# Threshold attention with a feed-forward block on one core: four moves in the order of loads, sums and means

## Chip, cores, metric

One core of a Trainium2 chip. The metric is the device time of one launch in microseconds, as the median of repeated runs.

## What is computed

The reference is attention with a threshold, followed by a layer norm and a feed-forward network with a residual. Cut to what matters (B = H = 8, S = 576, D = 64, model width 512, hidden width 2048):

```python
scores = matmul(q, k^T) / sqrt(64)
scores = where(scores >= max(scores) - tau, scores, -1e9)
attn   = softmax(scores)
x      = matmul(attn, v), heads side by side        # (8, 576, 512)
xn     = (x - mean(x)) / sqrt(var(x) + 1e-6) * g_ln
out    = x + relu(xn @ w_ch1) @ w_ch2
```

q, k, v are 32-bit floats. The two weight matrices come as 64-bit floats, and the kernel turns them into 32-bit ones on the chip.

## The kernel before

**Slots.** The work is cut into 72 slots, 9 for each batch, in one main loop over `n` (L1030 on). A slot of attention takes two heads and 256 of their 576 query rows (slots 0 to 3 of a batch the first 256, slots 5 to 8 the second); slot 4 takes what is left of all heads, the "shared heads". In each slot TensorE makes the scores of four blocks of 128 x 576 in PSUM (`scores`, L408), two blocks each in the tiles `sc0` and `sc1`. VectorE takes the maxima of the first two blocks and then of the other two (`exponentials`, L422); GpSimd makes a threshold from each (L426); ScalarE makes the exponentials (L436). `weights` (L443 and on) masks and sums them on VectorE. They are then turned round, in the first 9 slots by TensorE (`turn_weights`, tiles `tp`, `tr`), later by VectorE and a trip through DRAM (`turn_blocks`, L533, and `fetch`). The value products (`values_of`, L591, L601) follow one or two slots later, and ScalarE copies their result from PSUM to a tile `x` (L614, or L609 for the shared heads).

**Groups.** Each batch gives two groups of 288 tokens. GpSimd adds the features of `x` up as they come (`add_feature`, L643, tile `sum`); TensorE makes the mean by a product with a constant matrix (`mean_of`); VectorE subtracts it (`centre`, L666, tile `xc`). Then the group's feed-forward products begin: `first_part` (tile `p`, 16 times four products and a relu by ScalarE, L795), and the second half: for group 0 plainly (`second_plain`), for all others in seven half-size products of sums and differences (`second_quarters`, tile `seg`; VectorE and GpSimd make the sums, L865).

**Order.** The order of instructions on each engine's queue is the order in which the program issues them; it is written by hand. Every slot has points at which postponed calls run: -3, -2, -1 before the maxima, "copy", and the quarters 0 to 3. `at_quarter(n, i, ...)` puts a call at such a point and `run(n, i)` makes it. `second_part(n, i)` gives out feed-forward products, one at a time from a generator, as many as a share of the room (`ROOM`) allows. `group_ready` places a group's mean, centring and start: `ready(0)` is slot 6 quarter 0, `ready(1)` slot 10 quarter 2. The PSUM tiles of turnings, means and feed-forward products share one pool of two buffers.

**Loads.** All loads after the start are issued by SP in program order: `load_qk` (8 transfers of 72 KB, in pieces of 128 bytes; the single input buffer has to be free, so a load waits for the last transpose that reads it, L369), `load_v` (four transfers in batch 0), and the weight chunks. `Weights.fetch(most)` loads up to `most` of the 32 chunks of 512 KB, if room is free for them. Chunks are converted two per slot: VectorE (L271, L275, L298), ScalarE (L279, L283), GpSimd (L289, and L310 for the gain). `turn(u)` makes q and k ready for the scores: GpSimd scales q (L356), VectorE transposes k and q (L359, L363 or L368, L369). It stands behind the maxima of the slot before.

Of the kernel before, what the change touches and what calls it, by code (L numbers as in the profile page):

```python
# [18 lines left out]
def kernel(  # L19
# [36 lines left out]
    HP = H // 2  # L56
# [68 lines left out]
    def load_v(u):  # L125
        b, hp = units[u]
        vt = ins.tile([128, 2, J, D], F32, tag="v", name="v_in")
        vr = v_rest[hp]
        both = v[b, 2 * hp : 2 * hp + 2]
        if b:  # L130
            nc.sync.dma_start(
                out=vt.rearrange("p h c d -> p h (c d)"),
                in_=both[:, : J * 128].rearrange("h (p c) d -> p h (c d)", c=J),
            )
        for h in range(0 if b else 2):
            nc.sync.dma_start(
                out=vt[:, h], in_=both[h, : J * 128].rearrange("(c p) d -> p c d", p=128)
            )
        for j in range(2):
            nc.sync.dma_start(  # L140
                out=vr[64 * j : 64 * j + 64, j], in_=both[:, J * 128 :].rearrange("h p d -> p h d")
            )
        values_in[u] = (vt, vr)
# [270 lines left out]
    def exponentials(n):  # L414


        neg = small.tile([128, 4], F32, tag="neg", name="neg")
        thr = small.tile([128, 4], F32, tag="thr", name="thr")
        es = e_room[(n + 1) % 2 if n < SLOTS else 0]
        for h in range(2):  # L420
            i = slice(2 * h, 2 * h + 2)
            nc.vector.tensor_reduce(  # L422
                out=neg[:, i], in_=pairs[h],
                axis=AXL.X, op=ALU.max, negate=True,
            )
            nc.gpsimd.tensor_scalar(  # L426
                out=thr[:, i], in0=neg[:, i], scalar1=-1.0, scalar2=low_sb,
                op0=ALU.mult, op1=ALU.add,
            )
            if h == 0:  # L430
                conversion.scale_all()
        run(n, "copy")
        for i in range(4):
            if i == 2:
                yield es, thr
            nc.scalar.activation(es[:, i], blocks[i], func=AF.Exp, bias=neg[:, i : i + 1])  # L436
# [128 lines left out]
    def values_of(b, s, turned_weights):  # L565

        em, er = turned_weights
        at_once = b == 0 and s <= HP
        pv = pv_behind
        if at_once:  # L570
            both = ps_ff.tile([128, 2, 128], F32, tag="ff", name="pv")
            pv = [both[:, j] for j in range(2)]
        if s == HP:
            outs = [
                (hp, hp % 2, pv[hp % 2][:, hp // 2 * 64 : hp // 2 * 64 + 64],
                 lambda t, h, hp=hp: t[:, :, (2 * h + hp // 2) * 32 : (2 * h + hp // 2) * 32 + 32])
                for hp in range(HP)
            ]
        else:
            outs = [  # L580
                (s % (HP + 1), j, pv[j], lambda t, h: t[:, :, 64 * h : 64 * h + 64])
                for j in range(2)
            ]
        banks = [0 if at_once else j for _, j, _, _ in outs]
        firsts = [banks.index(bank) == i for i, bank in enumerate(banks)]
        lasts = [bank not in banks[i + 1 :] for i, bank in enumerate(banks)]
        for c in range(J):
            for (hp, j, dst, pick), first in zip(outs, firsts):
                vt, _ = values_in[b * HP + hp]
                for h in range(2):  # L590
                    nc.tensor.matmul(  # L591
                        dst[64 * h : 64 * h + 64], lhsT=vt[:, h, c, :],
                        rhs=pick(em[:, 2 * j : 2 * j + 2, c], h), start=c == 0 and first, stop=False,
                    )

        def rest():
            for (hp, j, dst, pick), last in zip(outs, lasts):
                _, vr = values_in[b * HP + hp]
                rows = slice(0, 128) if at_once else slice(64 * j, 64 * j + 64)
                for h in range(2):  # L600
                    nc.tensor.matmul(  # L601
                        dst[64 * h : 64 * h + 64], lhsT=vr[rows, j, h],
                        rhs=pick(er[rows], h), start=False, stop=last,
                    )

        def copy(j):
            if s == HP:
                for t in range(2):
                    nc.scalar.copy(  # L609
                        x_of(2 * b + t)[:, :, QH:].rearrange("p (a j) x -> p j a x", j=2)[:, j],  # L610
                        pv[j].rearrange("p (a t x) -> p t a x", a=2, t=2)[:, t],
                    )
            else:
                nc.scalar.copy(  # L614
                    x_of(2 * b + (s > HP))[:, s % (HP + 1), 128 * j : 128 * j + 128], pv[j]
                )

        def add():
            if s == HP:
                for t in range(2):  # L620
                    for c in range(1, NK):
                        add_feature(2 * b + t, c, slice(QH, TOK))
            elif s % (HP + 1):
                add_feature(2 * b + (s > HP), s % (HP + 1), slice(0, QH))

        if at_once:
            rest()
            copy(0)
            copy(1)
            add()  # L630
        else:
            n = b * SLOTS + s + 2
            at_quarter(n, -3, rest)
            at_quarter(n, -2, copy, 1)
            at_quarter(n, "copy", copy, 0)
            at_quarter(n, 0, add)

    def add_feature(g, c, cols):

# [7 lines left out]

    means, centred = {}, {}

    waiting_mean, banks_taken = [], [False]  # L650

    def mean_of(g):
        if banks_taken[0]:
# [289 lines left out]
    QUARTERS = 4  # L943
# [10 lines left out]
    def at_quarter(n, i, fn, *args):  # L954
        later_calls.setdefault((n, i), []).append((fn, args))

    def run(n, i):
        for fn, args in later_calls.pop((n, i), ()):
            fn(*args)

    def ready(g):

        if g < 2:
            return (24, 42)[g]
        b, t = divmod(g, 2)
        return QUARTERS * (b * SLOTS + (HP, 2 * HP)[t] + 2) + (2, 4)[t]

    def second_part(n, i):

        nonlocal issued, owed, part, now  # L970
        part, now = i, QUARTERS * n + i
        if not queue:
            return
        at = QUARTERS * n + i
        g = sum(issued >= e for e in ends)
        left = sum(ROOM[t % QUARTERS] for t in range(at, ready(g + 1))) if g + 1 < NG else 0
        owed += (ends[g] - issued) * ROOM[i] / left if left > 0 else 8


        got = 1 if i in (0, QUARTERS - 1) else 2  # L980
        while queue and (owed >= 0.5 or got == 1 and i in (0, QUARTERS - 1)):
            got, cost = next(queue[0], (None, 0))
            if got is None:
                queue.pop(0)
                got = 1
            elif got == 0:
                owed = 0.0
                break
            else:
                issued += cost  # L990
                owed -= cost

    def group_ready(g):
        first = divmod(ready(g), QUARTERS)
        before = divmod(ready(g) - 1, QUARTERS) if g else (first[0], -1)
        at_quarter(*before, mean_of, g)
        at_quarter(*(first if g and first[1] else before), centre, g)
        at_quarter(*first, lambda: queue.append(ffn_steps(g)))

    conversion = Weights()  # L1000
    if w_ch1.dtype == I64:
        conversion.fetch(4)
    else:
        for i in range(NK):
            nc.sync.dma_start(out=w1_sb[i], in_=w_ch1[i * 128 : (i + 1) * 128])
            nc.scalar.mul(w1_sb[i], w1_sb[i], g_sb[:, i : i + 1])
        for i in range(ND):
            nc.sync.dma_start(
                out=w2_sb[:, :, i],
                in_=w_ch2[i * 128 : (i + 1) * 128, :].rearrange("p (m c) -> p m c", m=NK),  # L1010
            )
        conversion.begun = conversion.carried = len(conversion.chunks)
        conversion.masked = conversion.fetched = conversion.begun
        conversion.scaled = conversion.n1
# [11 lines left out]

    constants(22)
    turn(0)
    load_v(1)
    for n in range(NS):  # L1030
        b, s = divmod(n, SLOTS)
        masks_at, behind_at, end_at = BEGUN[min(n, len(BEGUN) - 1)]
# [67 lines left out]
        if n >= HP + 2:  # L1100
            conversion.mask_all()
        run(n, 3)
        if b == 0 and s < HP - 2:
            load_v(s + 2)
        elif n >= SLOTS - 2 and (n + 2) % SLOTS < HP and n < NS - 2:
            load_v((n + 2) // SLOTS * HP + (n + 2) % SLOTS)
        second_part(n, 3)
# [44 lines left out]
```

## Time and profile before

| | |
|---|---|
| median of 3 runs | 1380.49 us (1380.27 to 1380.86) |
| profiled execution, its own time | 1383.39 us |
| its span, first to last instruction | 1381.4 us |
| VectorE busy | 919.6 us (67%) |
| GpSimd busy | 616.2 us (45%) |
| span of slots 0 to 9, from the first scores to those of slot 10 | 10.06 to 180.05 us |
| one batch later on | 159.1 us (450.6 to 609.7) |
| group 0: mean, first feed-forward product | 82.97, 88.79 us |
| group 1: mean, first feed-forward product | 187.53, 195.79 us |

The profile is one execution. A row of its timeline gives the start, the length, the engine, the line, the operation with the tile it writes and those it reads, how many records are merged in it, and in brackets how long the engine stood idle before it and what ended that. PE is TensorE (PEld its weight loads), DVE VectorE, ACT ScalarE, POOL GpSimd, SP the queue of loads and stores. A product here leaves four records (two halves of the output, each in two passes). Waits for several things are put down to the one that came last.

### The profile page before, as it was taken

The page shows a single profiled execution, that of the slowest core. Times are in us where ns is not written, and L with a number is a line of the kernel's source. Part 1 is how long each engine was busy: PE and PEld are TensorE (multiplying, and loading weights), DVE is VectorE, ACT ScalarE, POOL GpSimd, SP SyncE. Part 2 cuts the span into 40 slices and gives each one's busy share as a digit, 9 for nine tenths or more (in the row PEclk, how much of TensorE's full clock was granted, in tenths as well). Part 3 has the DMA queues.
Part 4 walks back from the last instruction along what each step waited for, and adds up shares of the span by engine and source line. Part 5 has one row for each costly group of instructions (what it writes and reads, how often), then busy time and mean ns, then how long its engine had stood idle before and what let it go on. Part 6 is the DMA issues. An engine that isn't in the chain of part 4 may idle for free.

```text
span 1381.4 us, 40994 instructions
## 1 busy us (share of the span) xinstructions
PE 1334.9 (97%) x17648; PEld 1008.5 (73%) x17648; DVE 919.6 (67%) x1638; ACT 455.1 (33%) x991; POOL 616.2 (45%) x823
## 2 busy tenths in 40 slices
PE   8989989999999999999999999999999999999996
PEld 6756655868778696867768687776868677786966
DVE  5888957676766777667766667657776767766211
ACT  3776523232323323232332323323232323323120
POOL 3464544544534454443444354343444445344313
PEclk9999999999999999999999999999999999999998
DMA  9722455447744576437744477445764476444211
GB/s 181 215 82 87 95 164 159 154 144 189 192 146 148 156 183 198 138 124 196 199 153 148 154 197 192 136 154 168 183 189 139 133 191 180 139 156 143 51 17 18
DMA packets 322020, 206.88 MB, mean 150 GB/s; under 512 B 247984, under 2 KB 279472, under 8 KB 313776
## 3 DMA queue, kind: packets, MB, share of 16 engines
q1 hardware_dynamic: 317072, 203.68, 50.5%
q8 instruction: 138, 2.26, 0.7%
q10 hardware_dynamic: 4736, 0.59, 0.4%
q14 instruction: 42, 0.34, 0.1%
q0 software_dynamic: 32, 0.00, 0.0%
HBM read 120.46 MB, written 83.76 MB: 148 GB/s over the span
## 4 chain that ended last, share of the span: by engine, by line
PE 84%; DVE 7%; ACT 2%; POOL 2%; issue 2%; DMA 2%; SPq 1%; POOLq 0%; DVEq 0%; ACTq 0%
PE p L101 35%; PE seg L101 28%; PE sc L408 9%; PE sc L591 8%; PE sc L601 2%; DVE neg L422 1%; DVE e L443 1%; PE tp L101 1%; DVE w L298 1%; ACT e L436 1%; DVE w L275 1%; PE mean L101 1%; POOL sum L643 1%; SPq L116 1%; POOL q_in L356 1%
## 5 line engine op out<-in xcount | busy, mean ns | idle before, releaser
L101 PE MATMUL p<-xc,w 128*64 128x288 f32 x4096 | 519.9, 409 | 14.1 <-ACT hidden L795 5.1
L101 PEld LDWEIGHTS p<-xc,w 128*64 128x64 f32 x4096 | 288.5, 137 | 223.2 <-issue 15.8
L422 DVE TENSOR_REDUCE neg<-sc 128x2 f32<-128x1152 f32 x144 | 188.6, 1351 | 237.5 <-PE sc L408 237.0
L101 PE MATMUL seg<-hidden,w 128*64 128x144 f32 x3840 | 248.3, 287 | 3.8 <-DVE hidden L865 3.8
L101 PEld LDWEIGHTS seg<-hidden,w 128*64 128x64 f32 x3840 | 234.9, 137 | 15.7 <-issue 7.5
L459 POOL TENSOR_SCALAR e<-e,den 128x576 f32<-128x576 f32 x252 | 193.8, 780 | 115.0 <-DVE den L448 114.7
L443 DVE SCALAR_TENSOR_TENSOR e<-sc,thr,e 128x576 f32<-128x576 f32 x288 | 222.0, 809 | 19.8 <-POOL thr L426 14.9
L426 POOL TENSOR_SCALAR thr<-neg,low_sb 128x2 f32<-128x2 f32 x144 | 42.1, 292 | 418.5 <-DVE neg L422 416.2
L795 ACT ACTIVATE hidden<-p 128x288 f32<-128x288 f32 x256 | 106.3, 416 | 325.2 <-PE p L101 323.5
L436 ACT ACTIVATE e<-sc,neg 128x576 f32<-128x576 f32 x288 | 197.6, 754 | 4.1 <-DVE neg L422 4.1
L533 DVE STREAM_TRANSPOSE et<-e 128x1152 f32<-128x1152 f32 x112 | 153.1, 1373 | 18.2 <-POOL e L459 17.7
L408 PE MATMUL sc<-kT,qT 64*64 64x384 f32 (+3 forms) x2048 | 140.8, 406 | 5.3 <-DVE e L443 5.1
L591 PE MATMUL sc<-em,v_in 128*64 128x128 f32 (+1 forms) x2368 | 129.5, 263 | 0.0
L591 PEld LDWEIGHTS sc<-em,v_in 128*64 128x64 f32 x2368 | 122.9, 137 | 7.8
L101 PE MATMUL seg<-hidden,stage 128*64 128x144 f32 x1920 | 123.3, 286 | 0.0
L101 PEld LDWEIGHTS seg<-hidden,stage 128*64 128x64 f32 x1920 | 117.6, 137 | 2.9 <-issue 2.9
L614 ACT COPY x<-sc 128x128 f32<-128x128 f32 x120 | 31.6, 265 | 241.5 <-PE sc L408 174.7
L408 PEld LDWEIGHTS sc<-kT,qT 64*64 64x64 f32 x2048 | 76.9, 134 | 47.0 <-issue 21.5
L865 POOL TENSOR_TENSOR hidden<-hidden 128x576 f32<-128x576 f32 x60 | 84.7, 1426 | 47.8 <-ACT hidden L795 38.2
L880 ACT COPY part<-seg 128x288 f32<-128x288 f32 x75 | 30.2, 403 | 198.4 <-PE seg L101 194.3
L865 DVE TENSOR_TENSOR hidden<-hidden 128x576 f32<-128x576 f32 x60 | 49.2, 854 | 49.1 <-PE seg L101 46.1
L101 PE MATMUL seg<-hidden,e 128*64 128x144 f32 x960 | 65.3, 286 | 0.0
(149 smaller groups left out, 1141.6 us busy)
## 6 DMA issues: line engine op xcount, KB each, us to landing
scr<-et SPq DMA_DIRECT2D x63, 1152.0 KB, 4.9
em<-scr SPq DMA_DIRECT2D x63, 1024.0 KB, 5.7
out_dram<-ot SPq DMA_DIRECT2D x256, 36.0 KB, 3.7
q_in<-in_q_dram SPq DMA_DIRECT2D x124, 72.0 KB, 2.5
k_in<-in_k_dram SPq DMA_DIRECT2D x120, 72.0 KB, 2.8
er<-scr SPq DMA_DIRECT2D x126, 64.0 KB, 5.2
v_in<-in_v_dram SPq DMA_DIRECT2D x28, 256.0 KB, 5.4
w<-in_moe_w_ch_dram SPq DMA_DIRECT2D x12, 512.0 KB, 5.5
```

The lines of the kernel that those rows point to most:

```text
L101: nc.tensor.matmul(out[r], lhsT=lhsT[:, r], rhs=rhs, **flags)
L408: nc.tensor.matmul(sc[h][64 * i : 64 * i + 64, at : at + n], lhsT=ql[r] if s == HP else qT[r, half, j * 128 + 64 * i : j * 128 + 64 * i + 64],
L422: nc.vector.tensor_reduce(out=neg[:, i], in_=pairs[h], axis=AXL.X, op=ALU.max, negate=True,)
L426: nc.gpsimd.tensor_scalar(out=thr[:, i], in0=neg[:, i], scalar1=-1.0, scalar2=low_sb, op0=ALU.mult, op1=ALU.add,)
L436: nc.scalar.activation(es[:, i], blocks[i], func=AF.Exp, bias=neg[:, i : i + 1])
L443: nc.vector.scalar_tensor_tensor(out=es[:, i], in0=blocks[i], scalar=thr[:, i : i + 1], in1=es[:, i], op0=ALU.is_ge, op1=ALU.mult, accum_o ...
L459: nc.gpsimd.tensor_scalar(out=es[:, i], in0=es[:, i], scalar1=den[:, i : i + 1], scalar2=1.0, op0=ALU.mult, op1=ALU.mult,)
L533: nc.vector.transpose(et[:, :, 64 * h : 64 * h + 64].rearrange("p n (j c) -> p j n c", j=2), es[:, 2 * h : 2 * h + 2].rearrange("p j (n c) ...
L591: nc.tensor.matmul(dst[64 * h : 64 * h + 64], lhsT=vt[:, h, c, :], rhs=pick(em[:, 2 * j : 2 * j + 2, c], h), start=c == 0 and first, stop= ...
L614: nc.scalar.copy(x_of(2 * b + (s > HP))[:, s % (HP + 1), 128 * j : 128 * j + 128], pv[j])
L795: nc.scalar.activation(hidden[:, d], p1, func=AF.Relu)
L865: eng.tensor_tensor(out=out[at], in0=in0[at], in1=in1[at], op=op)
```

## The change

It has four parts, and all of them change only where something stands in the order; what is computed stays the same.

- Loads: three weight chunks instead of four are fetched ahead of the loop, so that each later call fetches one chunk earlier in the list. The second v is loaded in slot 0 quarter 3 instead of ahead of the loop; the third and fourth v also come one slot later.
- Group 0's mean and centring move from point -1 of slot 6, ahead of the maxima, to quarter 0, behind them.
- The point "copy" moves from behind both maxima to behind the first maximum and its threshold, and the add of the features moves from quarter 0 to that point, behind the copy. On GpSimd the add so stands between the two thresholds.
- Group 1's mean and centring move to behind the fourth product of slot 10's quarter 1. Before, the mean stood ahead of that quarter's products and the centring behind the weights.

```diff
             if h == 0:
+                run(n, "copy")
                 conversion.scale_all()
-        run(n, "copy")
...
             at_quarter(n, "copy", copy, 0)
-            at_quarter(n, 0, add)
+            at_quarter(n, "copy", add)
...
-    waiting_mean, banks_taken = [], [False]
+    waiting_mean, banks_taken, among = [], [False], []
...
+        steps = 0
         got = 1 if i in (0, QUARTERS - 1) else 2
         while queue and (owed >= 0.5 or got == 1 and i in (0, QUARTERS - 1)):
...
                 issued += cost
                 owed -= cost
+                steps += 1
+                if steps == 4 and among:
+                    mean_of(among[0])
+                    centre(among.pop())
...
-        before = divmod(ready(g) - 1, QUARTERS) if g else (first[0], -1)
-        at_quarter(*before, mean_of, g)
-        at_quarter(*(first if g and first[1] else before), centre, g)
+        before = divmod(ready(g) - 1, QUARTERS) if g else first
+        if g == 1:
+            at_quarter(*before, lambda: among.append(g))
+        else:
+            at_quarter(*before, mean_of, g)
+            at_quarter(*(first if g and first[1] else before), centre, g)
...
-        conversion.fetch(4)
+        conversion.fetch(3)
...
     turn(0)
-    load_v(1)
...
-        if b == 0 and s < HP - 2:
-            load_v(s + 2)
+        if b == 0 and s < HP - 1:
+            load_v(s + 1)
```

## The prediction

> **What bounds the kernel now.** I read the page's busy shares first, then the chain of work that ended last, then the waits of TensorE, then the timelines of the four places where TensorE stands still and the change acts.
>
> ```profile
> PE 1334.9 (97%) x17648; PEld 1008.5 (73%) x17648; DVE 919.6 (67%) x1638; ACT 455.1 (33%) x991; POOL 616.2 (45%) x823
> PE 84%; DVE 7%; ACT 2%; POOL 2%; issue 2%; DMA 2%; SPq 1%; POOLq 0%; DVEq 0%; ACTq 0%
> ```
>
> TensorE is the bound: only 1381.4 - 1334.9 = 46.5 us of the span are without a matmul, and no edit here removes one. What can be won is idle time of TensorE and time at a lowered clock. In the table by stage a whole batch after the start (450.6 to 609.7) has 157.85 us of TensorE in 159.1, so most of it lies before 240 us. I number slots by the pass of the main loop; slots 0, 1, 2, 6, 10 and 19 start their scores at 10.06, 18.41, 33.80, 78.85, 180.05 and 660.42.
>
> The start, from the timeline of 0 to 38 us (start, length, engine, instruction, idle time before it):
>
> ```profile
> 16.71 0.20 DVE L369 STREAM_TRANSPOSE q_last<-q_in 128x64 f32<-128x64 f32 x1
> 17.75 5.64 SPq L116 DMA_DIRECT2D q_in<-in_q_dram  x4
> 23.44 2.12 SPq L116 DMA_DIRECT2D k_in<-in_k_dram  x4
> 28.48 0.78 DVE L359 STREAM_TRANSPOSE kT<-k_in 128x576 f32<-128x576 f32 x1 [3.79 <-DMA k_in<-in_k_dram]
> 33.80 0.86 PE L408 MATMUL sc<-kT,qT 64*64 64x384 f32 x4 [2.71 <-DVE e L443]
> 35.28 3.49 PE L408 MATMUL sc<-kT,qT 64*64 64x384 f32 x28 [0.61 <-DVE e L443]
> ```
>
> The third q, k are late: VectorE stands 3.79 us for k in slot 1, its weights come late, and the scores of slot 2 wait 2.71 + 0.61 us and then take 3.49 us where slot 1 has 2.16.
>
> Slot 10, where group 1's mean and centring stand:
>
> ```profile
> 186.75 0.72 POOL L643 TENSOR_TENSOR sum<-sum,x 128x256 f32<-128x256 f32 x1
> 187.53 0.71 PE L101 MATMUL mean<-sum,avg_sb 128*64 128x288 f32 x4 [2.79 <-POOL sum L643]
> 188.06 6.22 PE L101 MATMUL p<-hidden,w 128*64 128x288 f32 x36
> 195.79 4.59 PE L101 MATMUL p<-xc,w 128*64 128x288 f32 x36 [1.50 <-DVE xc L666]
> ```
>
> Three losses in a row: 2.79 us for the sum, 36 records in 6.22 us where the 36 below take 4.59, and 1.50 us for the centring.
>
> Slot 19, as an example of one stall per batch, and its row among the waits of TensorE (total, times, longest):
>
> ```profile
> 665.53 0.73 POOL L643 TENSOR_TENSOR sum<-sum,x 128x256 f32<-128x256 f32 x1
> 666.25 0.74 POOL L356 TENSOR_SCALAR q_in<-q_in,scl_sb 128x576 f32<-128x576 f32 x1
> 667.02 0.77 DVE L363 STREAM_TRANSPOSE qT<-q_in 128x256 f32<-128x256 f32 x2 [1.14 <-POOL q_in L356]
> 668.71 4.14 PE L101 MATMUL seg<-hidden,w 128*64 128x144 f32 x64 [0.63 <-DVE hidden L865]
> ```
> ```profile
> PE seg L101 <- DVE hidden L865: 3.8, 6, 0.6
> ```
>
> GpSimd does the sum, then the scaling of q; VectorE's transposes wait 1.14 us for it, and the operand of the fifth product (L865) is 0.63 us late. The chain of waits runs through exactly these steps.
>
> **What the Trainium skill says.** "TensorE: Matmul & The Clock Gate", What's actually happening: an idle window of about 3.4 us halves TensorE's clock until it has been busy as long. The trace agrees on the half (granted clock 0.50 in 36 to 38, 0.57 in 188 to 192) but shows it after gaps of only 2.71 + 0.61 and 2.79 us. "DMA: Bandwidth & Descriptors", Queues, rings and completion order: each DMA engine takes a queue's descriptors in ring order; the trace agrees in that the second and third q transfers take 2.57 and 1.81 us to issue while what was issued before drains. "PSUM — Partial Sum Buffer", PSUM bank collisions raise a hardware error: engines must not be in one bank at once. That is why the copy of the first half of x waits for the first maximum: 1.07 us in slot 19, from 663.96 on. Same page, Engine vs sequencer instructions: the queues of GpSimd and VectorE are strictly first in, first out, so each instruction moved delays or frees all behind it.
>
> **1. Loads.** Ahead of the third q, k go the fourth weight chunk (0.52 MB) and four transfers of v (0.32 MB). The q issue then waits only for L369 (ends 16.91) instead of 17.75: 0.75 us by issue alone. The backlog shrinks by 0.84 MB; at the 350 GB/s of 16 to 20 us that is 2.4 us. If the stalls go fully, eight issues of 0.5 us from 17.0 end at 21.1, and with the 2.9 us from the end of k's issue to the transpose k is there at 24.0, before VectorE's maxima end (24.68); then q's scaling (0.74, on GpSimd after the thresholds at 25.12) limits, and the transposes end 3.3 us earlier. I take the middle of 2.4 and 3.3: 2.9. TensorE's gap before slot 2 then nearly goes (its fill products end at 31.1, the scores could start at 30.9), so the clock should not fall, and 3.49 becomes 2.16; of that 1.3, VectorE gains what it waits beyond its own work, about 0.9. **Sum 3.8 us**, bounds 0.75 and 4.4. What is moved comes later: the fourth chunk and the first half of slot 0's fetch stand behind k's issue at about 22, land by the median 5.5 us at 28, and are wanted at 35.95 - 2.9 = 33; the second v is issued by 27 and wanted by slot 2's value products at 43.59 - 3.8. Third and fourth v go one slot later and keep a slot's margin. The next q, k stand behind the same number of bytes as now. SP's queue carries no other work there. Cost: nothing.
>
> **2. Group 0 (slot 6).** Mean and centring go from ahead of the maxima to behind them. Now TensorE waits 0.78 us for the sum, its four turnings are torn by the mean's PSUM bank, VectorE waits 1.32 us, and the first product stands at 88.79. After: turnings straight behind the scores (end 82.19); in slot 7 the last copy ends 4.35 us after the scores, so 86.54; mean 0.5, first subtraction 0.45, 0.14 to start: 87.7. **Gain 1.0 us.** Against it: VectorE idles from the maxima's end (85.1) to the mean and starts its weights 0.9 us later; their second half waits 2.63 us for exponentials today, which covers it. Bounds: a loss of 0.3 to a gain of 1.5.
>
> **3. Group 1 (slot 10).** Four of the 9 products of quarter 1 go ahead of the mean. They cover 4 x 4 x 0.12 = 1.9 us of the 2.79; the sum goes ahead of the second threshold, 0.7 us sooner (part 4), and covers the rest. So products to 186.4, mean 0.48, five more of 0.48: 189.3, with the pipe's end 189.6 instead of 194.28. The lowered clock (6.22 against 4.6 at the pace below) goes too. Centring then stands ahead of the weights on VectorE and starts behind the transposes and the mask of the last chunk, at about 189.8; the bank of the next product is free 0.5 us after 189.6. First product of group 1 at 190.2 instead of 195.79: **5.6 us**, bounds 4.0 (clock falls a little) and 6.3. VectorE's weights come 1.5 us later; the scores of slot 11 that overwrite their input stand at 203.78 - 5.6 = 198.2, weights end near 194.5. Slots 11 and 12 are a chain of VectorE from slot 11's maxima on, which wait for scores and so move along.
>
> **4. Sums (each later slot with features).** GpSimd's add goes between the two thresholds. In slot 19: first threshold 664.04, copy done 664.23, sum 664.35 to 665.08, second threshold at 665.30 as before, q's scaling at 665.53 instead of 666.25. VectorE gains 0.72, which covers the 0.63 that TensorE waits. Six times: **3.8 us**, bounds 0 and 4.4. Where copies are late (slot 8: 139.91) nothing is won. In the slot of the shared heads six small adds of 0.25 to 0.29 don't fit: the second threshold comes 0.77 us later, the weights with it (they wait for it 0.47 already), and the centring starts at 758.1 instead of 757.40; its product stands at 758.74 for a PSUM bank and needs 0.45 + 0.14 after that start, so it just fits. Cost taken 0, up to 0.5 in 7 batches.
>
> **Sum.** 3.8 + 1.0 + 5.6 + 3.8 = 14.2. From the profiled execution's 1383.39 that makes 1369.2; that execution is 2.9 above the median of the runs, so the median 1380.49 goes to **1366.3**.
>
> **Rivals.** (a) Issue of the third q, k keeps its pace (their 128-byte pieces, not the backlog, make the 2.57 and 1.81): part 1 gives 0.75, time 1369.3. For: even later issues take 0.5 us each; against: no other group has such stalls. (b) What slot 10 wins is handed back before slot 12, because VectorE and GpSimd (weight differences, L772) are behind there: TensorE waits 1.97 us at 228.49 and the clock falls again. Without part 3: 1371.9. For: the chain is VectorE's from 205.93 to 226.59; against: it begins at scores. (c) Another wait takes the place of L865 in each batch, since the weight load of the same product names a PSUM copy (0.86 us): without part 4, 1370.1. (d) **Slower:** every fetched chunk stands one place later, and VectorE, in order, stands still for each. Price 6.7 us a time, as at 182.36 where one late chunk holds it; four slots make 26.8, less the 14.2: 1393. It decides from 3.6 us a slot on; the margin is 5 us at median landing, and the longest landing of a chunk is 10.4, so it would need all four near the worst. (e) The chunk order happens to end the wait at 182.36: 1.6 us more, 1364.7.
>
> **Numbers.** Forecast 0.56, (a) 0.16, (b) 0.12, (c) 0.10, (d) 0.03, (e) 0.03. The range 1363 to 1372 holds all but (d) and mixtures. A measurement of this kernel can tell about 0.2% from no change (2.8 us); faster by more 0.94, within 0.03, slower 0.03.
>
> **What would show it.** Step 1: VectorE's wait for k in slot 1 under 1 us, slot 2's scores in 2.2 us. Step 2: first product of group 0 about 1 us nearer to slot 6's scores. Step 3: no wait of a mean for the sum, granted clock 1.00 in slot 10, first product of group 1 about 10 us after slot 10's scores start instead of 15.7. Step 4: the L865 wait of TensorE gone, VectorE's wait for q at 0.4 us. I am wrong if slots 3 to 9 become longer, or if second thresholds come later in ordinary slots.

## The result and the profile after

| | before | after |
|---|---|---|
| median | 1380.67 us (1380.27 to 1383.31, 4 runs) | 1367.22 us (1367.01 to 1368.69, 4 runs) |
| ratio, 95% interval | | 0.9901 [0.9884, 0.9918] |
| profiled execution, its span | 1383.39, 1381.4 us | 1367.01, 1365.0 us |

The kernel is 13.5 us (1.0%) faster; the forecast was 14.2. A second set of four runs of after, on another occasion, gave 1366.95 us and 0.9895 [0.9882, 0.9907].

From the page of after, the busy line and the shares of the chain that ended last:

```profile
PE 1330.1 (97%) x17648; PEld 1007.4 (74%) x17648; DVE 921.5 (68%) x1638; ACT 455.3 (33%) x991; POOL 616.7 (45%) x823
PE 88%; DVE 4%; ACT 3%; POOL 1%; issue 1%; DMA 0%; POOLq 0%; DVEq 0%; ACTq 0%; SPq 0%
```

TensorE now stands 1365.0 - 1330.1 = 34.9 us instead of 46.5; its busy time fell by 4.8 as well, at the same number of matmuls, because less of it ran at half clock. In the chain TensorE holds 88% instead of 84%, VectorE 4% instead of 7%.

The first scores of each slot cut both traces into stages:

| stage | before | after | gain | predicted |
|---|---|---|---|---|
| to slot 3 | 47.67 | 43.19 | 4.48 | 3.8 |
| slots 3 to 8 (group 0 in slot 6) | 108.35 | 107.59 | 0.76 | 1.0 |
| slot 9 | 24.03 | 24.72 | -0.69 | 0 |
| slot 10 (group 1) | 23.73 | 17.79 | 5.94 | 5.6 |
| slot 11 | 16.59 | 16.59 | 0 | 0 |
| slot 12 | 19.73 | 18.04 | 1.69 | 0 |
| slot 13 to the end | 1141.30 | 1137.08 | 4.22 | 3.8 |

They add up to 16.4, the difference of the two spans. The medians differ by only 13.5, and what lies between has to be explained too. Slot 9 alone became longer, by almost what slots 3 to 8 gained; slots 3 to 9 together stayed as long as they were (132.38 and 132.31 us).

The start of after, from the timeline:

```profile
17.09 3.09 SPq L116 DMA_DIRECT2D q_in<-in_q_dram  x4
20.23 2.12 SPq L116 DMA_DIRECT2D k_in<-in_k_dram  x4
24.71 0.77 DVE L359 STREAM_TRANSPOSE kT<-k_in 128x576 f32<-128x576 f32 x1
31.16 3.14 PE L408 MATMUL sc<-kT,qT 64*64 64x384 f32 x32
```

The issue of the third q (four transfers) takes 3.09 us instead of 5.64, k's transpose has no bracket any more (before: 3.79 us idle), and slot 2's scores begin right behind the fill products. They end at 34.30 instead of 38.77.

Slot 10 of after:

```profile
176.09 0.43 DVE L271 TENSOR_SCALAR stage<-x_room 128x512 uint32<-128x512 uint32 x1 [6.65 <-DMA x_room<-in_moe_w_ch_dram]
177.55 4.59 PE L101 MATMUL p<-hidden,w 128*64 128x288 f32 x36
179.75 0.72 POOL L643 TENSOR_TENSOR sum<-sum,x 128x256 f32<-128x256 f32 x1
181.97 0.66 PE L101 MATMUL mean<-sum,avg_sb 128*64 128x288 f32 x4
183.36 2.16 PE L101 MATMUL p<-hidden,w 128*64 128x288 f32 x16 [0.26 <-DVE w L298]
185.35 4.54 PE L101 MATMUL p<-xc,w 128*64 128x288 f32 x36
```

Nine products (36 records) run ahead of the mean where there were five (20 records), at full clock. The sum ends at 180.47, 1.5 us ahead of the mean that needs it. The first product of group 1 stands 9.85 us behind the slot's first scores (175.50), where before it was 15.74. VectorE still waits 6.65 us for the last weight chunk.

Slot 19 of after, and the row of its transposes among VectorE's waits:

```profile
650.42 8.16 PE L101 MATMUL seg<-hidden,w 128*64 128x144 f32 x128
650.81 0.73 POOL L643 TENSOR_TENSOR sum<-sum,x 128x256 f32<-128x256 f32 x1
651.99 0.74 POOL L356 TENSOR_SCALAR q_in<-q_in,scl_sb 128x576 f32<-128x576 f32 x1
652.76 0.77 DVE L363 STREAM_TRANSPOSE qT<-q_in 128x256 f32<-128x256 f32 x2 [0.45 <-POOL q_in L356]
```
```profile
DVE qT L363 <- POOL q_in L356: 14.5, 28, 1.7
```

The sum stands ahead of the second threshold (651.74), the transposes wait 0.45 us instead of 1.14, and 128 product records follow without a gap. Over the kernel that wait fell from 28.3 to 14.5 us; TensorE's wait for L865 (3.8 us) has no row any more.

### The profile page after: what moved, and what is told of

Its sections match the earlier page's. It is cut to its first block, busy times and chain, and to the rows that moved or that the text cites. A ratio compares the mean times of both kernels' runs of the same rounds, so it can differ in the third digit from the quotient of the medians.

```text
span 1365.0 us, 40999 instructions
## 1 busy us (share of the span) xinstructions
PE 1330.1 (97%) x17648; PEld 1007.4 (74%) x17648; DVE 921.5 (68%) x1638; ACT 455.3 (33%) x991; POOL 616.7 (45%) x823
## 4 chain that ended last, share of the span: by engine, by line
PE 88%; DVE 4%; ACT 3%; POOL 1%; issue 1%; DMA 0%; POOLq 0%; DVEq 0%; ACTq 0%; SPq 0%
PE p L101 35%; PE seg L101 31%; PE sc L408 10%; PE sc L591 8%; PE sc L601 2%; PE tp L101 1%; DVE e L443 1%; ACT e L436 1%; DVE w L298 1%; PE var L101 0%; PE mean L101 0%; DMA x_room<-in_moe_w_ch_dram 0%; DVE neg L422 0%; DVE et L533 0%; DVE w L275 0%
## 5 line engine op out<-in xcount | busy, mean ns | idle before, releaser
L436 ACT ACTIVATE e<-sc,neg 128x576 f32<-128x576 f32 x288 | 197.6, 754 | 4.1 <-DVE neg L422 4.1
L865 POOL TENSOR_TENSOR hidden<-hidden 128x576 f32<-128x576 f32 x60 | 84.8, 1427 | 51.9 <-ACT hidden L795 42.3
L865 DVE TENSOR_TENSOR hidden<-hidden 128x576 f32<-128x576 f32 x60 | 51.2, 887 | 49.1 <-PE seg L101 46.1
```

Source lines behind the costliest of these rows:

```text
L865: eng.tensor_tensor(out=out[at], in0=in0[at], in1=in1[at], op=op)
```

## The experiments

Lengths of stages in us, each from one profiled execution. "Ratio" is against the runs of before made beside the kernel (medians 1380.96, 1380.56 and 1381.04 in three sets), with its 95% interval.

| kernel | median | ratio | to slot 3 | slot 9 | slot 10 | slot 12 | 13 to end |
|---|---|---|---|---|---|---|---|
| before | 1380.67 | | 47.67 | 24.03 | 23.73 | 19.73 | 1141.3 |
| before again | 1382.89 (1 run) | | 47.29 | 24.03 | 23.72 | 19.74 | 1141.2 |
| loads only | 1376.13 | 0.9971 [0.9960, 0.9982] | 43.09 | 24.75 | 21.19 | 19.74 | 1141.3 |
| sums only | 1374.63 | 0.9953 [0.9935, 0.9971] | 46.57 | 24.02 | 20.97 | 19.74 | 1137.1 |
| group 1 only | 1377.07 | 0.9974 [0.9967, 0.9982] | 45.31 | 24.02 | 20.01 | 18.04 | 1141.3 |
| group 0 only | 1378.53 | 0.9989 [0.9980, 0.9997] | 47.52 | 24.03 | 22.29 | 19.74 | 1141.3 |
| v only | 1378.08 | 0.9985 [0.9977, 0.9992] | 44.33 | 24.03 | 22.27 | 18.06 | 1141.3 |
| chunk only | 1376.15 | 0.9972 [0.9962, 0.9981] | 44.22 | 24.81 | 21.16 | 19.75 | 1141.3 |
| after without group 1 | 1369.18 | 0.9922 [0.9907, 0.9937] | 43.16 | 24.73 | 20.01 | 18.06 | 1137.2 |
| fill before slot 2 | 1379.40 | 0.9993 [0.9985, 1.0000] | 44.91 | 24.02 | 22.25 | 18.05 | 1141.3 |
| after, four chunks | 1368.45 | 0.9904 [0.9891, 0.9916] | 43.09 | 24.02 | 18.79 | 19.73 | 1137.2 |
| after, shared adds back | 1367.00 | 0.9899 [0.9884, 0.9914] | 43.10 | 24.73 | 17.78 | 18.05 | 1137.2 |
| after again | 1366.95 | 0.9895 [0.9882, 0.9907] | 43.08 | 24.76 | 17.82 | 18.04 | 1137.1 |

My theory was the prediction's sum, each part acting in its own place. The rivals were that parts share the same time, so that some of it is counted twice, and that part of what the profile of before shows belongs to that one execution.

**Before again** (no edit).

> The kernel before, unchanged, profiled a second time. Theory 1 (the two profiles differ by the change alone): the span is 1381.4 us again and the 52 records of slot 12's feed-forward products take 8.2 us at half clock, as in the first profile. Theory 2 (the first profile of before holds clock losses that most executions don't have, about 2.9 us, the distance of its 1383.4 from the median 1380.5): the span is about 1378.5, those 52 records take 6.5 us as after the change, and one of the other places at half clock (slot 2, slot 10) may also differ.

The second execution has the same three stretches of slow products: 3.85 us for slot 2's 28 score records, 6.22 for 36 records in slot 10, 8.21 for 52 in slot 12. So theory 1 held here; one execution more says little on how often.

**Loads only.**

```diff
-        conversion.fetch(4)
+        conversion.fetch(3)
...
-    load_v(1)
...
-        if b == 0 and s < HP - 2:
-            load_v(s + 2)
+        if b == 0 and s < HP - 1:
+            load_v(s + 1)
```

> Only the loads are moved (three chunks ahead of the loop, second v in slot 0). Theory 1 (each part acts at its place): 4.5 us less up to slot 7, where the trace after the change has 4.47, and nothing later: 1376.2. Theory 2 (the shift by one chunk also changes when the last chunks are converted, so that slot 9 loses 0.7 and slot 10's maxima are no longer held up by the last chunk, which brings the sum 1.6 us sooner): 1373.5 to 1375.5, with the mean's wait in slot 10 at about 1.2 us instead of 2.79.

The start gains all of its 4.6 us here already (47.67 to 43.09). The prediction had nothing later. But slot 9 becomes 0.7 us longer and slot 10 2.5 shorter, 1.5 of it the clock, which stays full there (36 records in 4.54 us); the mean's wait for its sum is 1.8 us instead of 2.8. The median, 1376.13, is theory 1's, the stages are nearer to theory 2, but the last chunk still holds up slot 10's maxima (VectorE waits 6.69 us for it), only less far into the slot.

**v only, chunk only** (each half of the edit above by itself).

> Only the loads of v are moved, four chunks stay ahead of the loop. Theory 1 (backlog in bytes: v is 0.32 of the 0.84 MB that go): about 40% of the start's gain, VectorE's wait for k in slot 1 at 2 us instead of 3.79, time 1378.5. Theory 2 (the number of pieces counts, not the bytes: v's 256-byte rows are most of the pieces ahead of q, k): nearly the whole gain, wait under 0.5 us, 1376.2, and no shift of the later chunks, so that slot 9 is as before.

> Only the fourth chunk is moved, v stays ahead of the loop. Theory 1 (bytes): 60% of the start's gain, wait for k at 1.5 us, plus the effect in slots 9 and 10: 1376 to 1378. Theory 2 (pieces): little at the start, wait for k above 3 us; what is left is the effect of the shifted chunks, slot 9 longer by 0.7 and slot 10's maxima right behind the scores: 1378 to 1380.

From the timeline of v only, then of chunk only:

```profile
19.20 5.04 SPq L116 DMA_DIRECT2D k_in<-in_k_dram  x4
26.47 0.78 DVE L359 STREAM_TRANSPOSE kT<-k_in 128x576 f32<-128x576 f32 x1 [1.72 <-DMA k_in<-in_k_dram]
```
```profile
17.20 4.82 SPq L116 DMA_DIRECT2D q_in<-in_q_dram  x4
26.36 0.78 DVE L359 STREAM_TRANSPOSE kT<-k_in 128x576 f32<-128x576 f32 x1 [1.63 <-DMA k_in<-in_k_dram]
```

With either half k's transpose starts at about 26.4, against 27.05 to 28.48 in the executions with all loads in their old place, and an issue stall stays with either: it moves from q to k when v is gone. The waits, 1.72 and 1.63 us, are near what theory 1 (bytes) said for each half. What lies ahead of the transfers matters, then, which speaks against rival (a), their own 128-byte pieces, the same in all three kernels. But 0.32 and 0.52 MB give about the same, and k's arrival varies by more than a microsecond between executions of the same loads: after with four chunks, below, has the loads of v only up to here, and its k is waited for by 0.57 us alone, as little as theory 2 (pieces) said. Whether bytes or pieces count, and how much each, stays open.

The change of slots 9 and 10 belongs to the chunk alone: 24.81 and 21.16, against 24.03 and 22.27 with v only.

**Sums only.**

```diff
             if h == 0:
+                run(n, "copy")
                 conversion.scale_all()
-        run(n, "copy")
...
-            at_quarter(n, 0, add)
+            at_quarter(n, "copy", add)
```

> Only the adds are moved between the thresholds. Theory 1: six stalls of 0.63 to 0.70 us go, 4.0 us, and the mean of group 1 waits 0.7 us less: 1375.8. Theory 2 (the adds matter only together with the other parts, since something else is late next): 1378 to 1380, with a wait of TensorE for L865 still in the slots 19, 28, ...

Theory 1 held in the later slots: they gain 4.2 us, all that after gains there. Slot 19 is 18.08 us long instead of 18.78, and so is the same slot of the five batches behind it. In slot 10 the mean waits 1.3 us instead of 2.8, a gain of twice the 0.7 expected.

**Group 1 only.**

```diff
+                steps += 1
+                if steps == 4 and among:
+                    mean_of(among[0])
+                    centre(among.pop())
...
+        if g == 1:
+            at_quarter(*before, lambda: among.append(g))
...
```

> Only group 1's mean and centring are moved among the products. Theory 1 (this move alone takes out most of slot 10's losses): the mean waits 1.1 us for the sum instead of 2.79, the clock stays up, first product of group 1 near 191.2 instead of 195.8: 4.6 us, 1375.9. Theory 2 (the gain of slot 10 needs the earlier sum): the clock still falls after the mean and the gain is 2.5 us or less, 1378.

From TensorE's timeline of slot 10 in this kernel:

```profile
185.17 0.71 PE L101 MATMUL mean<-sum,avg_sb 128*64 128x288 f32 x4 [0.85 <-POOL sum L643]
187.76 2.16 PE L101 MATMUL p<-hidden,w 128*64 128x288 f32 x16 [1.40 <-DVE w L298]
```

The move by itself takes 3.7 us off slot 10 as the profile of before has it, between what the two theories said. The wait for the centring is gone and that for the sum is short, but a new one stands behind the mean: 1.40 us for the conversion of the last weight chunk (L298), which VectorE ends behind the late maxima and the transposes. The prediction had that step of VectorE ahead of the centring, but no product that waits for it.

**Group 0 only.**

```diff
-        before = divmod(ready(g) - 1, QUARTERS) if g else (first[0], -1)
+        before = divmod(ready(g) - 1, QUARTERS) if g else first
```

> Only group 0's mean and centring are moved behind the maxima. Theory 1: first product of group 0 stands 0.74 us sooner after slot 6's scores, as in the trace after the change, and all of it stays: 1379.8. Theory 2 (the chain from slot 7 to 10 is VectorE's and a late chunk's, so that the gain is lost before slot 10): 1380.5, with slot 10's scores at the same place as before.

Slots 3 to 8 shrink from 108.35 to 107.57 us, as in after. The medians lie 2.0 us apart, but the interval, 0.4 to 2.8 us, also holds the 0.8 that the stages show. In this profile slot 10 is 22.29 although the mean waits 2.86 us, because the products behind it keep their pace.

**After without group 1** (after with the mean and the centring of group 1 where they were before).

```diff
-        if g == 1:
-            at_quarter(*before, lambda: among.append(g))
-        else:
-            at_quarter(*before, mean_of, g)
-            at_quarter(*(first if g and first[1] else before), centre, g)
+        at_quarter(*before, mean_of, g)
+        at_quarter(*(first if g and first[1] else before), centre, g)
```

> The changed kernel with group 1's mean and centring back at their old places. Theory 1 (that move is worth the 5.6 us put down to it): 1372.8. Theory 2 (earlier sums and the earlier last chunk already bring the sum 2.4 us forward, so the mean waits only 0.4 us and the clock stays up; only the late centring is left): 1.5 to 2.5 us, 1368.7 to 1369.7.

Theory 2 held: 1369.18 us, and the mean waits only 0.3. With the other parts in place the move is worth 2.2 us in slot 10 (20.01 to 17.79), not 5.6.

**Fill before slot 2.**

```diff
-            constants(8 if n > 1 else 26)
+            constants(26 if n == 1 else 20 if n == 2 else 8)
```

> The kernel before with 12 more fill products ahead of slot 2's scores (20 instead of 8), on a tile that nobody reads. Theory 1 (slot 2's slow scores are a lowered clock, brought on by TensorE's idle gap ahead of them): the gap shrinks to under 1.4 us, the 28 score records take 2.16 us instead of 3.5 to 3.85, slot 3 starts about 1.5 us sooner (46 instead of 47.3 to 47.7), and the median goes from 1380.6 to about 1379.2. Theory 2 (the scores are slow since k and q arrive piece by piece): the records stay at 3.5 or more, and the time at 1380.6.

All 32 score records of slot 2 now take 2.37 us, from 33.63 on, and slot 3 starts at 44.91. Of the 2.8 us to before, 1.4 is k, which came that much earlier in this execution (27.05 against 28.48); the rest is the clock, which stayed up. The median fell by 1.6 us, with an interval that just touches no change. So theory 1 holds in the profile: without the gap the clock stays up. That a gap brings it down each time doesn't hold, as group 1 only shows (a gap of 1.60 + 0.61 us there, and 2.16 us for the records). The same execution gives the plainest contrast with before. TensorE's rows of slot 10:

```profile
184.99 0.71 PE L101 MATMUL mean<-sum,avg_sb 128*64 128x288 f32 x4 [2.82 <-POOL sum L643]
185.53 4.54 PE L101 MATMUL p<-hidden,w 128*64 128x288 f32 x36
```

and two stretches of 2 us behind the mean in the table by stage, first of before, then of this kernel (TensorE's busy time and records come first; the granted clock stands behind GpSimd's):

```profile
188.00:190.00 2.00, 2.00 (x12) 1.02 (x10) 1.76 (x6) 0.00 (x0) 0.20 (x1) 0.55 0.01 2
```
```profile
185.00:187.00 2.00, 2.00 (x18) 1.21 (x20) 1.30 (x5) 0.46 (x1) 0.67 (x1) 1.00 0.03 8
```

The same wait, the same code, and once 0.55 of the clock and 6.22 us for the 36 records, once 1.00 and 4.54. The last section shows what differs.

**After, four chunks** (after with `conversion.fetch(4)`).

> The kernel after with four weight chunks instead of three fetched ahead of the loop; the moved v stays. Theory 1 (the shifted chunk order costs 0.7 us in slot 9 and wins about 1.6 us in slot 10, since the last chunk then no longer holds the maximum): slot 9 back to 24.0 us from 24.7, slot 10 at 19 to 19.4 us from 17.79, the start as good within 0.7 us; time 1368 to 1369.5. Theory 2 (the order of the chunks matters only at the start): slots 9 and 10 at 24.7 and 17.8, time 1367.4.

Slot 9 goes back to 24.02 and slot 10 to 18.79: the order of the chunks costs 0.7 in one and gives 1.0 in the other. VectorE's rows ahead of slot 9's maxima, of after (slot from 150.78) and then of this kernel (from 150.69):

```profile
153.18 1.70 DVE L275 SCALAR_TENSOR_TENSOR stage<-stage 128x512 uint32<-128x512 uint32 x1
155.19 2.58 DVE L422 TENSOR_REDUCE neg<-sc 128x2 f32<-128x1152 f32 x2
```
```profile
153.03 2.58 DVE L422 TENSOR_REDUCE neg<-sc 128x2 f32<-128x1152 f32 x2
```

In after a second chunk is begun ahead of the maxima, which start 2.1 us later. The last chunk is converted 6.5 us after its issue in both (169.56 to 176.09, and 169.75 to 176.31) and waited for as long; since slot 10 starts later in after (175.50 against 174.71), the wait lies beside more of its scores. So in slots 9 and 10 the chunk order is worth about 0.3 us. At the start this execution is as good as after (43.09 and 43.19), but that of v only, with the same loads, had k 1.25 us later and slot 3 at 44.33, while the five profiles with both parts of the loads moved all lie at 43.08 to 43.19. The median, 1.2 us higher than after's, doesn't divide this: the profiled run, 1368.80, has slot 12's longer form, 19.73, and a later k would add about as much.

**After, shared adds back.**

```diff
-            at_quarter(n, "copy", add)
+            at_quarter(n, 0 if s == HP else "copy", add)
```

> The kernel after with the six small adds of the shared heads' slot back behind both thresholds, the adds of all other slots left where they are. Theory 1 (part 4 costs nothing in the shared heads' slot, as predicted): within 0.5 us of the kernel after, 1366.7 to 1367.7. Theory 2 (the second threshold, 0.77 us later, is paid in each of seven batches): 3 to 5 us faster, 1362 to 1364. Theory 3 (the adds are needed early there too): slower, 1369 or more.

Theory 1 held: 1367.00 us, and the later slots 1137.2 as in after. The rows of the first weights, the second threshold and the centring in after, in one shared slot, then the centring in this kernel, whose slot stands 0.07 us earlier:

```profile
739.78 0.82 DVE L443 SCALAR_TENSOR_TENSOR e<-sc,thr,e 128x576 f32<-128x576 f32 x1 [0.47 <-ACT e L436]
740.16 0.27 POOL L426 TENSOR_SCALAR thr<-neg,low_sb 128x2 f32<-128x2 f32 x1
743.14 1.52 DVE L666 TENSOR_TENSOR xc<-x,mean 128x288 f32<-128x288 f32 x4
```
```profile
743.07 1.52 DVE L666 TENSOR_TENSOR xc<-x,mean 128x288 f32<-128x288 f32 x4
```

The second threshold does come 0.8 us later (it is at 739.34 here), but neither the weights nor the centring move. In before the row of the same weights was

```profile
754.04 0.82 DVE L443 SCALAR_TENSOR_TENSOR e<-sc,thr,e 128x576 f32<-128x576 f32 x1 [0.47 <-POOL thr L426]
```

The wait is 0.47 us in both, put down once to the threshold and once to the exponential (L436). So it was the exponential's all along. The first two blocks of weights read only the first threshold; the third, which needs the second, starts at 741.46 in after, 1.0 us behind its end.

**After again** (no edit).

> The kernel after once more, unchanged, beside the three others. Theory 1 (slot 12 falls to the lowered clock in some executions and not in others, with the same 1.97 us gap ahead): its length in this profile is either 18.05 or 19.7 us with all else as in the first profile of after, and the runs spread over about 1.7 us or more; median 1367.2. Theory 2 (the four parts together keep the clock up there): 18.05 us, and the runs stay within 1 us.

Its four runs lie within 0.1 us, as theory 2 said, and slot 12 takes 18.04 us. But one run of the first set stood at 1368.69, and the two kernels next to after have runs at 1368.7 to 1368.8, so theory 1 fits the whole better. TensorE's rows of slot 12, of after and then of after with four chunks:

```profile
218.00 6.53 PE L101 MATMUL p<-xc,w 128*64 128x288 f32 x52 [1.97 <-ACT hidden L795]
```
```profile
218.20 8.22 PE L101 MATMUL p<-xc,w 128*64 128x288 f32 x52 [1.97 <-ACT hidden L795]
```

Over all 14 profiles the gap is 1.96 to 1.98 us; seven have 8.21 or 8.22 us behind it and seven 6.53.

## Why the prediction was right, and where it wasn't

**The total** was 1366.3 against 1367.22, inside the range. In the profiled executions it was 1369.2 against 1367.01. The gain of 14.2 is too small for the profiles (16.4) and too large for the medians (13.5), largely because I took what the profile of before shows in slots 2 and 10 as lasting. That execution had the lowered clock in three places (1.3 to 1.7 us each, 4.7 in all). The runs of before spread over 6 us (1376.95 to 1383.04 in one set of 27), and their granted clock tells why. Of 106 such runs, those with a mean clock of 0.997 have a median of 1377.4 us, with 0.996 1379.1, with 0.994 1380.9 and with 0.993 1382.6: steps of 1.7 to 1.8 us, as none, one, two or three losses make them (eight runs at 0.995 lie between). Seven of the eight runs of after stand at 0.997, at 1366.9 to 1367.4. So about 10.4 of the 13.5 us are there without any loss of the clock, and about 3 come from losses that before has more often. Two of the three places are mended by the change: none of the four profiles with all the loads and the sums moved has a slow stretch there. The third, in slot 12, isn't, and in the profile of after its products kept their pace by the luck of one execution. That the total came within 0.9 us of the median is luck in part: I counted losses of 0.9 and 1.6 us in slots 2 and 10 as certain and none in slot 12; all three come and go, and what before has of them on average is about as much.

**1. Loads**, 4.5 instead of 3.8. The mechanism held: k is hardly waited for (0 to 0.43 us in the five profiles with both parts of the loads moved), and the scores start behind the fill. Both terms came out at the upper end: q's last transposes end 3.1 us earlier (I took 2.9, between 2.4 and 3.3), and VectorE's wait for slot 2's scores, 1.32 us ahead of its maxima, is gone (I took 0.9). But this is one pair of executions: the five profiles with the old loads and the old fill have slot 3 at 45.31 to 47.67, 46.9 on average, which makes 3.8. That the mean falls on my figure is chance; the stall is not one size. Rival (a) fell. "Cost: nothing" for the shifted chunks was wrong in form: they cost 0.7 in slot 9 by VectorE's own work ahead of the maxima, which I looked for only as waits. Slot 10 gives it back with 0.3 over. My own sign of being wrong, longer slots 3 to 9, came in slot 9 and not in their sum. Rival (e) fell too: the 6.7 us wait is still there. Rival (d) fell: VectorE waits for no chunk but the last.

**2. Group 0**, 0.76 instead of 1.0. From the timeline of slot 6 in before, then in after:

```profile
82.97 0.71 PE L101 MATMUL mean<-sum,avg_sb 128*64 128x288 f32 x4 [0.78 <-POOL sum L643]
83.79 1.55 DVE L666 TENSOR_TENSOR xc<-x,mean 128x288 f32<-128x288 f32 x4 [1.32 <-PE mean L101]
```
```profile
82.17 0.71 PE L101 MATMUL mean<-sum,avg_sb 128*64 128x288 f32 x4 [0.31 <-ACT em L493]
82.98 1.55 DVE L666 TENSOR_TENSOR xc<-x,mean 128x288 f32<-128x288 f32 x4 [2.46 <-PE mean L101]
83.58 6.77 PE L101 MATMUL p<-xc,w 128*64 128x288 f32 x54 [0.71 <-ACT e L436]
```

The first product stands 9.20 us behind the first scores (74.38), where before it was 9.94 and I had 8.85. The mean stands 7.79 us behind them, where I had 7.69. The mis-sized term is "mean 0.5": the subtraction starts 0.81 us after the mean, and the trace of before had shown that (82.97 to 83.79).

**3. Group 1**, 5.94 instead of 5.6: right as a total, wrong in its shares. Take the three executions with the old order in slot 10 and a full clock (group 0 only, v only, fill before slot 2), 22.27 us. Chunk order alone takes 1.1 from them, sums alone 1.3, the move alone 2.25. That makes 4.65, and after is 4.5 below them. The remaining 1.5 of the 5.94 is the lowered clock, which both profiles of before have there and these three don't. I had put the clock and the whole 5.6 to the move, and used the earlier sum without saying that it gains by itself. Also missed is the wait for L298, 1.4 us with the move alone and 0.26 in after, where the maxima come sooner against the slot and the transposes wait 0.5 us for q instead of 1.1, so that VectorE ends the last chunk sooner. The marks named in the prediction came out: no wait of the mean for the sum, full clock, first product at 9.85 us. Rival (b) fell: slot 11 is 16.59 in both.

**4. Sums**, 4.2 instead of 3.8: each stall was worth 0.70, not the 0.63 that the bracket shows. In the shared slot the cost was nothing, as taken, but not by the path that I gave. I read VectorE's wait of 0.47 us as one for the second threshold, and so had the weights and the centring come 0.7 us later and "just fit"; it was a wait for the exponential, and neither moved. Rival (c) fell: no other wait takes the place of L865.

## What to carry to other kernels

Look at more than one execution before costing a stall: whether the clock is lost behind a gap changes from execution to execution, so count it by the runs, not by the one profile. Where several edits meet in one place, cost each with the others in place; here the move of group 1 showed 3.7 us alone against the profile of before, and 2.2 in the end. And when loads change order, follow the work that they feed, not only whether they arrive in time.

## What the runs showed of the hardware

**TensorE's clock changes on a grid of 3.41 us.** The 14 profiles have 13 stretches at half clock inside the kernel, and each is 3.41 us long; within one execution all changes of the clock lie whole multiples of 3.41 us apart. Where the grid lies differs from execution to execution. The table by stage, cut at the grid in slot 12 of before and then of after (TensorE's busy time comes first, the granted clock behind GpSimd's):

```profile
225.76:229.17 3.41, 1.44 (x14) 0.63 (x11) 3.41 (x5) 2.58 (x6) 1.50 (x3) 1.00 0.66 181
229.17:232.58 3.41, 3.41 (x18) 1.71 (x14) 3.34 (x11) 1.23 (x3) 2.17 (x4) 0.50 0.76 208
```
```profile
216.46:219.87 3.41, 1.87 (x16) 1.18 (x18) 3.41 (x6) 3.05 (x6) 1.85 (x2) 1.00 0.55 168
```

Both have the same gap of 1.97 us. In before (226.52 to 228.49) it lies within one stretch of the grid, which has 1.44 us of TensorE, and the next stretch runs at half clock. In after (216.03 to 218.00) the grid cuts the gap, the stretch has 1.87 us of TensorE, and the clock stays up. Each of the 13 follows a stretch of the grid with at most 1.48 us of TensorE. Of the others, over 5400, a single one has less than 1.52 (1.41, in slot 10 of fill before slot 2). So what looks like chance is, by this reading, where a gap falls on a grid that the kernel doesn't set. No run moved the grid; only in slot 2 was the gap itself filled, and the clock stayed up. An estimate from these figures: a little more of TensorE's work in slot 12's gap, enough to take 1.44 us above 1.52, would save 1.7 us in about half of the executions (7 of 14). It was not tried.

- Each loss in slots 10 and 12 cost 1.7 us (6.22 - 4.54, 8.21 - 6.53), as half of 3.41 us should. Gaps of 1.96 to 1.98 us in slot 12 were followed by one in seven of 14 executions, gaps of 2.79 to 2.86 in slot 10 in two of five, gaps of 1.35 to 2.71 (with 0.61 behind) in slot 2 in four of five. The Trainium skill, "TensorE: Matmul & The Clock Gate", What's actually happening, says that the idle window of about 3.4 us runs free, so that where a change of the clock falls differs from run to run. The traces agree with both. They don't agree that a whole window must be idle: those ahead of a loss had 0.68 to 1.48 us of TensorE.
- SP took 4.41 to 5.64 us to issue the third q (four transfers of 72 KB) in the six executions with a chunk and v just ahead of it. With v gone and the chunk still ahead, q took 2.12 and 2.39 us in two executions, and k behind it 5.04 and 3.71.
